# Dilated window attention and a maxout feed-forward layer: one unit of the second batch, not four, turned by TensorE, steps of scores and values taken apart, and a first tile that opens on three chunks of four

## The chip, the cores and the metric

The kernel runs on one core of one Trainium2 chip. The metric is the time of one execution on the device in microseconds (us). Beside it stands one execution taken by the hardware profiler, with a trace of every instruction on the five engines: TensorE (PE in the profile, its weight loads apart as PEld), VectorE (DVE), ScalarE (ACT), GpSimd (POOL) and SyncE (SP), which here only issues DMAs.

## The reference, cut to what matters

```python
# q, k, v: [8 batches, 8 heads, 576 positions, 64]; 4 heads plain, 4 dilated
scores = q @ k.T / 8
rel = pos[:, None] - pos[None, :]
mask_plain = (rel >= 0) & (rel < 32)                       # heads 0-3
mask_dil = (rel >= 0) & (rel < 128) & (rel % 4 == 0)       # heads 4-7
attn = softmax(where(mask, scores, -1e9))                  # denominator + 1e-9
x = (attn @ v) with the heads side by side                 # [8*576 = 4608, 512]
h = max(x @ w1, x @ w2, x @ w3)                            # 512 -> 768
out = h @ w_out                                            # 768 -> 512
```

All is float32. Only a band of scores counts, 32 keys per query, so the kernel computes small blocks beside the diagonal.

## The kernel before, in words

**The feed-forward layer.** The 4608 tokens are cut into nine tiles of 512. Each number is kept as a high part in the fp32r format and a low remainder, and each product is made of three (`ffn`, L957): high weights by high x, high weights by low x, low weights by high x. A tile has 18 "up" groups (six blocks `f` of 128 hidden columns, three weights each). A group is 12 matmuls into one PSUM bank `u`: three steps of four matmuls, one for each 128-row chunk of x (L979 to L987). The four chunks are the four pairs of heads. VectorE takes the maximum over the three groups (`tmp`), ScalarE rounds it to `h`, GpSimd makes the remainder. Then 72 "down" matmuls into the banks `d` (L1034) give four blocks of 128 tokens. So a tile is 216 up and 72 down matmuls of 512 columns.

**The weights** come once. `weight` (L394) loads an up group (512 KB) or half a down block (256 KB) into a staging tile `st`, and ScalarE, GpSimd and VectorE make the high and low parts `wupH`, `wupL` and `wdn` from packed bytes (L456 to L483).

**Attention** works in units: batch `b`, pair of heads `p` (0 and 1 plain, 2 and 3 dilated), 32 in all. There are two ways to make one:

- `full(b, p)` (L488), used for the first `NPAIR * FULL` = 8 units, the two first batches. TensorE writes the mask into the score banks `fs` with four matmuls of an identity (L553) and adds 36 or 48 score products (L559). VectorE takes row maxima (L576), and for the first head of the pair the subtraction (L579) and the sum (L585) too; ScalarE makes the exponentials (L582, L599); GpSimd normalises `W`. TensorE turns `W` in three steps of transposes (`ft`, L643 and L667), ScalarE copies the result out (`PT`), and 36 or 48 products with the values (`fpv`, L689) give x.
- `attention(u)` (L765) with `behind` (L814), for the other 24. 40 or 48 score products (`s`, L801), mask, maximum and shift in one custom VectorE operation for each of ten blocks (L830), exponentials and sums on ScalarE (L842), normalising on GpSimd, and 12 or 16 VectorE transposes of 32x32 blocks (L891). 32 products with the values (`pv`, L929) follow.

In both, x is copied to `xH` and its remainder to `xL` (ScalarE and VectorE). In the second way, `products` (L940) makes one TensorE step of the values of a unit and the scores of the next (`unit`, L1075), so the two stand side by side on TensorE.

**The order of all work** is computed when the kernel is built, by `Plan` (L104). Each step has a cost for each engine that may do it. `deadlines` gives each a due time, counted back from the feed-forward steps, which are numbered through at a pace; `order` (L171) then always takes the step that can begin first, by due time among those, and so fixes each engine's queue. Engines work their queues strictly in that order. TensorE steps of the first tile wait for all four chunks of x of batch 0. While TensorE would wait, `filler` matmuls (`idle`, L1116) are put in before the first feed-forward step; one of the two banks tagged `ffn` serves them until then, and the first value bank of every `full` unit has that tag too (L681). Loads stand in SP's queue by the same rule, the two `k` buffers in turn; the third unit of the first batch has its keys and queries in spare `h` buffers.

A tile needs x of all units of its tokens: the first tile batch 0, the second batches 0 and 1, and so on. The units of batch 1 are therefore worked on while the first tile runs.

Of the kernel before, what the change touches and what calls it, by code (L numbers as in the profile page):

```python
# [21 lines left out]
HALF = 288  # L22
# [24 lines left out]
FILL = 0.22  # L47
PER_BLOCK = 0.146
BACKLOG = 4.0
WEIGHT_PACE, WEIGHT_SLACK, WEIGHT_LEAD = 0.3, 3.188, 0.8  # L50

# [39 lines left out]
class Step:  # L91


    def __init__(self, costs, fn, bufs, nbytes, rows, kind, lead):
        self.costs, self.fn, self.bufs, self.nbytes, self.rows = costs, fn, bufs, nbytes, rows
        self.kind, self.lead = kind, lead
        self.usual = self.eng = next(iter(costs))
        self.next = []
        self.left = 0
        self.goal = self.due = 0.0  # L100
        self.ready = dict.fromkeys(costs, 0.0)


class Plan:  # L104
# [10 lines left out]
    def __init__(self):  # L115
        self.steps, self.made, self.given = [], {}, {}
        self.kind, self.lead = None, 0.0

    def add(self, costs, fn, deps=(), bufs=(), nbytes=0, rows=128):
# [51 lines left out]
    def order(self, fill=None):  # L171
# [14 lines left out]
        while len(order) - fills < len(self.steps):  # L186
            best = None
            for e, cands in waiting.items():
                now = free[e]
                for st in cands:  # L190
                    at = max(now, st.ready[e], wire - BACKLOG if e == "sp" else 0.0)
                    if best is not None and at > best[0]:
                        continue
                    if st.bufs:
                        at = max(at, self.room(st, slots))
                    if best is not None and (at, st.due) >= best[:2]:
# [10 lines left out]
                    best = (at, st.due, e, st)  # L207
            at, _, e, st = best
            assert at < 1e9, "the steps wait for each other's buffers"
            if e == "pe" and st.kind == "ffn" and len(slots["ffn"]) < 2 and fill:  # L210
                fill = None
# [67 lines left out]
def tile_dilated_window_attention__then__maxout_ffn(  # L279
# [114 lines left out]
    def weight(j, before):  # L394
# [56 lines left out]
        def sign(_):  # L451
# [36 lines left out]
    def full(b, p):  # L488
# [5 lines left out]
        top = 64 + nq  # L494
        at_h = not b and p == 2
        kb = buf("h" if at_h else "k", f"fk{b}{p}", [128, 1024] if at_h else None, F32)
# [13 lines left out]
        if at_h:  # L510
            ks = plan.add(*load(kb, qk[b, p % 2, :, 576:], 128, nkc))
            qs = plan.add(*load(qb, qk[b, p % 2, :, :576], 128, 576))
        else:
            ks = qs = plan.add(*load(kb, qk[b, p % 2], 128, 576 + nkc))
        if b:
# [31 lines left out]

        def scores(_):

            for j in range(2):  # L550
                for i, g in enumerate((slice(0, 4 * dil or 1), slice(4 * dil or 1, G))):
                    m = steps[:, i : i + 1, :wk].broadcast_to([128, g.stop - g.start, wk])
                    nc.tensor.matmul(S3(j)[:, g], identb, m, start=not i, stop=False, skip_group_check=True)  # L553
            for n, (r, i) in enumerate(blocks):
                q0, k0 = 144 * r + nq * i, ko + kw * r + nq * i
                for j in range(2):
                    d = slice(64 * j, 64 * j + 64)
# [9 lines left out]

        s = plan.add({"pe": 0.6 + 1.05}, scores, [ks, qs, first_of[b]], [*{kb, qb}, mx, *banks])
        expd = []
        for j, bank in enumerate(banks):  # L570
# [20 lines left out]

            t = plan.add({"dve": dve(nw)}, most, [s], [bank, mx])
            if byblock:
# [41 lines left out]
        for j in range(2):  # L635
# [21 lines left out]
            normed.append(t)  # L657
            t = plan.add({"pe": 4 * gw / 600 + 0.05}, flip, [t], [W, flips[j], *PT])
            copied.append(plan.add({"act": act(8 * nq), "dve": dve(8 * nq)}, moved, [t], [flips[j], PT[j]]))
# [8 lines left out]

        s = plan.add({"pe": (4 * gw if dil else 2 * nq) / 600 + 0.05}, rest, normed, [W, flips[2]])
        for j in range(2):  # L670
# [28 lines left out]
        for z in range(2):  # L699
# [20 lines left out]
            ls.append(l)  # L720
        return [(2 * HALF * b, 2 * HALF * b + 2 * HALF, hs, ls)]

    def rounded_of(b, p, dil, pv):

        def rounded(s):
            out = []
            for z, (c0, c1) in enumerate(((0, 256), (256, 2 * HALF))):
# [4 lines left out]
                for a, e in ((x0, wrap), (wrap, x1)):  # L732
# [26 lines left out]
                    ls.append(l)  # L759
                out.append((x0, x1, hs, ls))  # L760
            return out
# [3 lines left out]
    def attention(u, after):  # L765
# [30 lines left out]
        def scores():  # L796
# [11 lines left out]

        cost = sum(nq * SCORE for _, _, nq, *_ in blocks)
        return (scores, cost, [kload], [kb, mx, W, *banks]), (  # L810
            lambda s: behind(u, name, s, blocks, banks, W, mx, sm, v, vloads)
        ), (kload, last)

    def behind(u, name, s, blocks, banks, W, mx, sm, v, vloads):  # L814
# [40 lines left out]
        blank = [None, None]  # L855
        if u < NPAIR * FULL + 2:
            blank = [
# [78 lines left out]

        cost = 4 * (2 * HALF / 2400 + 8 * 0.0105)
        return values, cost, [*vloads, *turned[0], *turned[1]], [*v, *PT, *pv], rounded_of(b, p, dil, pv)

    def products(units, scores=()):  # L940
# [3 lines left out]
        def run(_):  # L944
# [3 lines left out]
        s = plan.add(  # L948
            {"pe": sum(x[1] for x in parts) + 0.25},
            run,  # L950
# [6 lines left out]
    def ffn(t0, n, x_of, w_of, prev):  # L957
# [12 lines left out]

        hs, hsteps = [], []
        for f in range(NF):
            tmp, hb = buf("tmp", f"tmp{t0}_{f}"), buf("h", f"h{t0}_{f}")
            for g in range(3):
                bank = buf("ffn", f"u{t0}_{f}_{g}")
                terms = ((wupH, 0, 0), (wupH, 0, 1), (wupL, 1, 0))
                for m, (wt, wz, xz) in enumerate(terms):

                    def up(_, m=m, wt=wt, xz=xz, f=f, g=g, bank=bank):  # L979
                        for c in range(4):  # L980
                            nc.tensor.matmul(  # L981
                                sums(bank),
                                wt[:, 3 * f + g, c, :],
                                moving(xL if xz else xH, c),
                                start=(m == 0 and c == 0),
                                stop=(m == 2 and c == 3),
                            )  # L987

                    prev = plan.add(
                        {"pe": 4 * (n * 0.000425 + 0.01)},  # L990
                        up,
                        [
                            prev,
                            *(x for a in x_of if a[0] < t0 + n and a[1] > t0 for x in a[2 + xz]),
                            w_of[3 * f + g][wz],
                        ],
                        [bank],
                    )
                if g == 0:
# [75 lines left out]
    def unit(u):  # L1075
# [109 lines left out]
```

## Time and profile before

| | us |
|---|---|
| median of 3 runs | 710.59 (709.3 to 713.65) |
| the profiled execution, its own time | 709.76 |
| its span, first to last instruction | 708.0 |
| TensorE busy in the span | 697.6 |
| VectorE, ScalarE, GpSimd busy | 330.9, 251.9, 178.7 |

A row of a timeline or of the chain has the start, the duration, the engine, the line, the tiles (`out<-in`) and the number of instructions merged. A row of a table of stretches has, for each engine, busy time and number of instructions, then the granted clock of TensorE as a share of full speed, the share of the DMA engines and GB/s. Ends of matmuls are modelled: what a matmul costs in a stream is read from one start to the next. "idle before <-releaser" names what ended a wait.

### The profile page before, as it was taken

The page shows a single profiled execution, that of the slowest core. Times are in us where ns is not written, and L with a number is a line of the kernel's source. Part 1 is how long each engine was busy: PE and PEld are TensorE (multiplying, and loading weights), DVE is VectorE, ACT ScalarE, POOL GpSimd, SP SyncE. Part 2 cuts the span into 40 slices and gives each one's busy share as a digit, 9 for nine tenths or more (in the row PEclk, how much of TensorE's full clock was granted, in tenths as well). Part 3 has the DMA queues.
Part 4 walks back from the last instruction along what each step waited for, and adds up shares of the span by engine and source line. Part 5 has one row for each costly group of instructions (what it writes and reads, how often), then busy time and mean ns, then how long its engine had stood idle before and what let it go on. Part 6 is the DMA issues. An engine that isn't in the chain of part 4 may idle for free.

```text
span 708.0 us, 13566 instructions
## 1 busy us (share of the span) xinstructions
PE 697.6 (99%) x5253; PEld 565.2 (80%) x5253; DVE 330.9 (47%) x1188; ACT 251.9 (36%) x875; POOL 178.7 (25%) x236
## 2 busy tenths in 40 slices
PE   9989999999999999999999999999999999999997
PEld 5668778888888888888888888888888888888886
DVE  6889754565555554513455544555455301101110
ACT  5857743333333333312433333334333211111111
POOL 3666752122112221211122211221122101100120
PEclk9999999999999999999999999999999999999999
DMA  9991822221221213100321032112200010010001
GB/s 298 330 375 58 243 72 106 75 61 64 89 92 62 65 64 119 59 1 24 137 80 57 11 109 77 59 62 94 92 26 1 16 44 1 0 45 16 0 1 59
DMA packets 23407, 57.42 MB, mean 81 GB/s; under 512 B 3056, under 2 KB 4784, under 8 KB 23344
## 3 DMA queue, kind: packets, MB, share of 16 engines
q1 hardware_dynamic: 23344, 56.57, 24.2%
q8 instruction: 41, 0.67, 0.4%
q14 instruction: 22, 0.18, 0.1%
HBM read 47.12 MB, written 9.44 MB: 80 GB/s over the span
## 4 chain that ended last, share of the span: by engine, by line
PE 92%; DMA 4%; POOL 2%; DVE 1%; issue 1%; ACT 0%; SPq 0%; POOLq 0%; ACTq 0%
PE u L981 61%; PE d L1036 21%; PE pv L929 4%; PE s L801 3%; DMA fk<-in_qk_p_dram 1%; DMA st<-in_w_dn_dram 1%; DMA st<-in_w_up_dram 1%; POOL W L371 1%; PE fpv L689 1%; PE fs L559 0%; PE idle L1117 0%; POOL wdn L371 0%; DVE fmx L576 0%; PE ft L643 0%; POOL c L438 0%
## 5 line engine op out<-in xcount | busy, mean ns | idle before, releaser
L981 PE MATMUL u<-xH,wupH 128*128 128x512 f32 x648 | 176.3, 394 | 2.0 <-ACT tmp L347 1.8
L981 PE MATMUL u<-xL,wupH 128*128 128x512 f32 x648 | 174.8, 391 | 0.0
L371 DVE TENSOR_TENSOR tmp<-u,tmp 128x512 f32<-128x512 f32 x108 | 74.5, 690 | 213.8 <-PE u L981 207.7
L981 PE MATMUL u<-xH,wupL 128*128 128x512 f32 x648 | 173.8, 390 | 0.0
L1036 PE MATMUL d<-wdn,h 128*128 128x512 f32 x648 | 151.4, 391 | 0.0
L371 POOL TENSOR_TENSOR h<-tmp,h 128x512 fp32r<-128x512 f32 x54 | 69.8, 1293 | 310.9 <-ACT h L347 310.6
L981 PEld LDWEIGHTS u<-xH,wupH 128*128 128x128 f32 x648 | 121.0, 189 | 28.4 <-ACT tmp L347 2.3
L981 PEld LDWEIGHTS u<-xH,wupL 128*128 128x128 f32 x648 | 121.4, 188 | 25.5
L981 PEld LDWEIGHTS u<-xL,wupH 128*128 128x128 f32 x648 | 121.2, 188 | 25.6
L1036 PEld LDWEIGHTS d<-wdn,h 128*128 128x128 f32 x648 | 120.8, 188 | 25.9
L891 DVE STREAM_TRANSPOSE PT<-W 32x256 f32<-32x256 f32 (+1 forms) x336 | 117.7, 350 | 27.8 <-POOL W L371 21.9
L842 ACT ACTIVATE W<-W,mx 128x96 f32<-128x96 f32 (+2 forms) x240 | 85.6, 359 | 38.1 <-DVE mx L830 38.1
L347 ACT CAST h<-tmp 128x512 fp32r<-128x512 f32 x54 | 33.5, 621 | 183.9 <-DVE tmp L371 183.9
L830 DVE CUSTOM_DVE_ANT_0 W<-s,steps 128x96 f32<-128x96 f32 x192 | 37.1, 253 | 58.5 <-PE s L801 58.5
L347 ACT COPY tmp<-u 128x512 f32<-128x512 f32 x54 | 31.7, 587 | 62.3 <-POOL h L371 34.4
L371 POOL TENSOR_TENSOR W<-W,sm 128x768 f32<-128x768 f32 (+2 forms) x48 | 44.2, 920 | 34.5 <-DVE sm L876 34.5
L347 ACT COPY o<-d 128x512 f32<-128x512 f32 x36 | 21.2, 588 | 79.9 <-PE d L1036 77.8
L842 ACT ACTIVATION_READ_ACCUMULATOR W<-W,mx 128x1 f32 (+1 forms) x240 | 45.3, 189 | 0.0
L871 POOL TENSOR_TENSOR sm<-sm,small_c 128x8 f32<-128x8 f32 (+2 forms) x48 | 9.4, 195 | 136.0 <-ACT W L842 136.0
L347 ACT CAST xH<-pv 128x320 fp32r<-128x320 f32 (+3 forms) x46 | 16.3, 381 | 65.5 <-PE pv L929 47.5
L929 PEld LDWEIGHTS pv<-PT,v 96*64 96x64 f32 (+2 forms) x768 | 26.3, 137 | 8.5 <-issue 6.7
L929 PE MATMUL pv<-PT,v 96*64 96x64 f32 (+2 forms) x768 | 29.9, 230 | 0.0
(70 smaller groups left out, 408.8 us busy)
## 6 DMA issues: line engine op xcount, KB each, us to landing
st<-in_w_up_dram SPq DMA_DIRECT2D x18, 512.0 KB, 9.0
out_dram<-o SPq DMA_DIRECT2D x36, 256.0 KB, 2.0
k<-in_qk_d_dram SPq DMA_DIRECT2D x12, 640.0 KB, 4.2
k<-in_qk_p_dram SPq DMA_DIRECT2D x12, 592.0 KB, 4.5
st<-in_w_dn_dram SPq DMA_DIRECT2D x12, 256.0 KB, 4.8
v<-in_vb_p_dram SPq DMA_DIRECT2D x12, 256.0 KB, 4.3
v<-in_vb_d_dram SPq DMA_DIRECT2D x12, 224.0 KB, 4.3
fk<-in_qk_p_dram SPq DMA_DIRECT2D x4, 592.0 KB, 7.3
```

The lines of the kernel that those rows point to most:

```text
L347: nc.scalar.copy(dst, src)
L371: (nc.vector if eng == "dve" else nc.gpsimd).tensor_tensor(dst, a, b, op=op)
L689: nc.tensor.matmul(pv[z].t[64 * j : 64 * j + 64, c : c + nq], value(n, j), PT[j].t[:wk, x : x + nq], start=True, stop=True,)
L801: nc.tensor.matmul(banks[j].t[o : o + nq, 96 * m : 96 * m + nk], kb.t[d, q0 : q0 + nq], kb.t[d, k0 : k0 + nk], start=True, stop=True,)
L830: nc.vector.tensor_tensor_reduce(W.t[:rows, a], banks[j].t[:rows, 96 * m : 96 * m + nk], tails[:rows, :nk] if m == 4 else steps[:, 0 if di ...
L842: nc.scalar.activation(W.t[:rows, a], W.t[:rows, a], AF.Exp, bias=mx.t[:rows, n : n + 1], scale=-1.0, accum_out=sm.t[:rows, n : n + 1],)
L871: nc.gpsimd.tensor_tensor(d, d, eps_c[:rows].broadcast_to([rows, n]), op=ALU.add)
L891: plan.add({"dve": dve(32 * n) + 0.02}, lambda _: nc.vector.transpose(dst(), src()), [*deps, blank[z]], [W, PT[z]])
L929: nc.tensor.matmul(pv[z].t[64 * j : 64 * j + 64, q0:q1], v[z].t[:rows, j, m, :], rows_of(z)[:rows, 4 * j + m, : q1 - q0], start=True, stop ...
L981: nc.tensor.matmul(sums(bank), wt[:, 3 * f + g, c, :], moving(xL if xz else xH, c), start=(m == 0 and c == 0), stop=(m == 2 and c == 3),)
L1036: nc.tensor.matmul(bank.t, hs[f].t[:, hz, s0 : s0 + 128], wdn[f].t[:, wz], start=(f == 0 and m == 0), stop=(f == NF - 1 and m == 2),)
```

## The change

It has four parts.

1. `FULL_UNITS = 5` takes the place of `NPAIR * FULL` = 8: only unit 0 of batch 1 still goes through `full`. Units 5, 6 and 7 (pairs 1, 2 and 3 of batch 1) are made as the later ones are.
2. `ALONE = 10`: for units 5 to 9 the values are a TensorE step of their own, and not joined with the next unit's scores.
3. `PORDER = (2, 0, 1, 3)`: in batch 0 the dilated pair 2 comes first. Its keys and queries come as two transfers of 64 partitions each, one for each head, and each head's scores are a step of their own that waits for its half alone. Pair 1 is now the one in the `h` buffers. The first two up groups of the first tile are made of the chunks 2, 0 and 1 first (nine matmuls each), and of chunk 3 later (three each), so they can begin before pair 3 is done; the step that opens the feed-forward layer takes the second `ffn` bank, and the value banks of batch 1 and of pair 3 no longer have the `ffn` tag. Chunks are summed in the order 2, 0, 1, 3 everywhere.
4. The planner: the first three up weights get a fixed due time (`RANK_ST`), a step that could begin up to `HOLD` later may be preferred by due time, and most costs and paces have new values.

The diff, cut to its core (the steps' new names `ups`, `early` and `scored` are at the places named above):

```diff
-SPILL = 1.67
+SPILL = 1.342
-SCORE = 0.00105
-FFN_PACE = 1.044
-UNIT_PACE, UNIT_SLACK, UNIT_LEAD = 1.271, 7.676, 3.484
+SCORES, VALUES = 1.06, 1.14
+FFN_PACE = 1.081
+UNIT_PACE, UNIT_SLACK, UNIT_LEAD = 1.319, 7.676, 3.484
-PER_BLOCK = 0.146
-BACKLOG = 4.0
-WEIGHT_PACE, WEIGHT_SLACK, WEIGHT_LEAD = 0.3, 3.188, 0.8
+PER_BLOCK = 0.131
+FLIP = 0.00088
+BACKLOG = 4.768
+HOLD = 0.102
+WEIGHT_PACE, WEIGHT_SLACK, WEIGHT_LEAD = 0.204, 3.188, 0.509
...
+FULL_UNITS = 5
+PORDER = (2, 0, 1, 3)
+FIRST_ST, RANK_ST = 3, -27.563
+EARLY = PORDER
+ALONE = 10
...
-            st.goal = st.due = g - k * dur
+            st.goal = g - k * dur
+            st.due = st.goal if st.rank is None else st.rank
...
+        if j < FIRST_ST:
+            s.rank = RANK_ST + j
...
+            for d in ([slice(0, 64), slice(64, 128)] if first_unit else [slice(0, 128)]):
+                def keys_in(_, d=d):
+                    nc.sync.dma_start(out=kb.t[d, : 576 + nkc], in_=qk[b, p % 2, d])
...
+        if first_unit:
+            scored = [plan.add({"pe": 0.25 + 1.1}, lambda _, j=j: scores([j]), [heads[j]], [kb, mx, banks[j]]) for j in range(2)]
...
-        pv = [buf("b" if i else "ffn", f"fpv{b}{p}_{i}") for i in range(2)]
+        pv = [buf("b" if i or b or p == PORDER[3] else "ffn", f"fpv{b}{p}_{i}") for i in range(2)]
...
-        if u < NPAIR * FULL + 2:
+        if u < FULL_UNITS + 2:
             blank = [
...
+        def ups(f, g, bank, chunks, opens=False):
+            for m, (wt, wz, xz) in enumerate(((wupH, 0, 0), (wupH, 0, 1), (wupL, 1, 0))):
+                def up(_, m=m, wt=wt, xz=xz):
+                    for c in chunks:
+                        nc.tensor.matmul(
...
+                            start=(m == 0 and c == EARLY[0]),
+                            stop=(m == 2 and c == EARLY[3]),
...
+        ahead = 2 if not t0 else 0
+        early = [buf("ffn", f"u{t0}_0_{g}") for g in range(ahead)]
+        for g, bank in enumerate(early):
+            ups(0, g, bank, EARLY[:3], g == 1)
...
+                if f == 0 and g < ahead:
+                    bank = early[g]
+                    ups(f, g, bank, EARLY[3:])
...
         made = [rest(s)] if new else []
+        if u < ALONE:
+            for r in products(made)[1]:
+                x_of.extend(r())
+            made = []
...
-                if u < NPAIR * FULL:
+                if u < FULL_UNITS:
                     plan.lead = UNIT_LEAD * (NPAIR - 1 - p)
-                    x_of.extend(full(u // NPAIR, p))
+                    x_of.extend(full(u // NPAIR, p if u >= NPAIR else PORDER[p]))
                 else:
-                    if u == NPAIR * FULL:
+                    if u == FULL_UNITS:
                         unit(u)
                     unit(u + 1)
```

More of the change, by code (lines that the diff above doesn't have):

```diff
@@ L100, in __init__ @@
         self.goal = self.due = 0.0
+        self.rank = None
         self.ready = dict.fromkeys(costs, 0.0)
@@ L188, in order @@
             for e, cands in waiting.items():
-                now = free[e]
+                now, found, soon = free[e], [], 1e9
                 for st in cands:
                     at = max(now, st.ready[e], wire - BACKLOG if e == "sp" else 0.0)
-                    if best is not None and at > best[0]:
+                    if at > soon + HOLD:
                         continue
-                    if st.bufs:
+                    if st.bufs and not (fill and st is self.opener):
                         at = max(at, self.room(st, slots))
-                    if best is not None and (at, st.due) >= best[:2]:
+                    if at > soon + HOLD:
                         continue
@@ L206, in order @@
                             continue
-                    best = (at, st.due, e, st)
+                    soon = min(soon, at)
+                    found.append((st.due, at, st))
+                found = [x for x in found if x[1] <= soon + HOLD]
+                if found:
+                    due, at, st = min(found, key=lambda x: x[:2])
+                    if best is None or (at, due) < best[:2]:
+                        best = (at, due, e, st)
             at, _, e, st = best
             assert at < 1e9, "the steps wait for each other's buffers"
-            if e == "pe" and st.kind == "ffn" and len(slots["ffn"]) < 2 and fill:
+            if st is self.opener and fill:
                 fill = None
@@ L494, in full @@
         top = 64 + nq
-        at_h = not b and p == 2
+        at_h, first_unit = not b and p == PORDER[2], not b and p == PORDER[0]
         kb = buf("h" if at_h else "k", f"fk{b}{p}", [128, 1024] if at_h else None, F32)
@@ L511, in full @@
             ks = plan.add(*load(kb, qk[b, p % 2, :, 576:], 128, nkc))
+            heads = []
             qs = plan.add(*load(qb, qk[b, p % 2, :, :576], 128, 576))
         else:
-            ks = qs = plan.add(*load(kb, qk[b, p % 2], 128, 576 + nkc))
+            ks = qs = None
+            heads = []
+            for d in ([slice(0, 64), slice(64, 128)] if first_unit else [slice(0, 128)]):
+                def keys_in(_, d=d):
+                    nc.sync.dma_start(out=kb.t[d, : 576 + nkc], in_=qk[b, p % 2, d])
+                heads.append(plan.add({"sp": 0.5}, keys_in, (), [kb], (d.stop - d.start) * (576 + nkc) * 4))
         if b:
@@ L546, in S3, with scores @@
             return banks[j].t[:, :nw].rearrange("p (n k) -> p n k", k=wk)
-        def scores(_):
-            for j in range(2):
+        def scores(js):
+            for j in js:
                 for i, g in enumerate((slice(0, 4 * dil or 1), slice(4 * dil or 1, G))):
@@ L555, in scores @@
                 q0, k0 = 144 * r + nq * i, ko + kw * r + nq * i
-                for j in range(2):
+                for j in js:
                     d = slice(64 * j, 64 * j + 64)
@@ L566, in scores @@
                     )
-        s = plan.add({"pe": 0.6 + 1.05}, scores, [ks, qs, first_of[b]], [*{kb, qb}, mx, *banks])
+        if first_unit:
+            scored = [plan.add({"pe": 0.25 + 1.1}, lambda _, j=j: scores([j]), [heads[j]], [kb, mx, banks[j]]) for j in range(2)]
+        else:
+            scored = 2 * [
+                plan.add({"pe": 0.47 + 1.08}, lambda _: scores(range(2)), [ks, qs, *heads, first_of[b]], [*{kb: 0, qb: 0}, mx, *banks])
+            ]
         expd = []
@@ L590, in eighth @@
                 )
-            t = plan.add({"dve": dve(nw)}, most, [s], [bank, mx])
+            t = plan.add({"dve": dve(nw)}, most, [scored[j]], [bank, mx])
             if byblock:
@@ L657, in full @@
             normed.append(t)
-            t = plan.add({"pe": 4 * gw / 600 + 0.05}, flip, [t], [W, flips[j], *PT])
+            t = plan.add({"pe": 4 * gw * FLIP + 0.06}, flip, [t], [W, flips[j], *PT])
             copied.append(plan.add({"act": act(8 * nq), "dve": dve(8 * nq)}, moved, [t], [flips[j], PT[j]]))
@@ L667, in rest @@
                     nc.tensor.transpose(flips[2].t[:wk, c : c + rows], W3(j)[:rows, g], ident[:rows, :rows])
-        s = plan.add({"pe": (4 * gw if dil else 2 * nq) / 600 + 0.05}, rest, normed, [W, flips[2]])
+        s = plan.add({"pe": (4 * gw if dil else 2 * nq) * FLIP + 0.06}, rest, normed, [W, flips[2]])
         for j in range(2):
@@ L759, in rounded @@
                     ls.append(l)
-                out.append((x0, x1, hs, ls))
+                out.append((x0, x1, p, hs, ls))
             return out
@@ L807, in scores @@
                     )
-        cost = sum(nq * SCORE for _, _, nq, *_ in blocks)
-        return (scores, cost, [kload], [kb, mx, W, *banks]), (
+        return (scores, SCORES, [kload], [kb, mx, W, *banks]), (
             lambda s: behind(u, name, s, blocks, banks, W, mx, sm, v, vloads)
@@ L935, in values @@
                         )
-        cost = 4 * (2 * HALF / 2400 + 8 * 0.0105)
-        return values, cost, [*vloads, *turned[0], *turned[1]], [*v, *PT, *pv], rounded_of(b, p, dil, pv)
+        return values, VALUES, [*vloads, *turned[0], *turned[1]], [*v, *PT, *pv], rounded_of(b, p, dil, pv)
     def products(units, scores=()):
@@ L948, in products @@
         s = plan.add(
-            {"pe": sum(x[1] for x in parts) + 0.25},
+            {"pe": sum(x[1] for x in parts) + 0.05},
             run,
@@ L971, in ffn @@
         hs, hsteps = [], []
+        def ups(f, g, bank, chunks, opens=False):
+            nonlocal prev
+            j = 3 * f + g
+            for m, (wt, wz, xz) in enumerate(((wupH, 0, 0), (wupH, 0, 1), (wupL, 1, 0))):
+                def up(_, m=m, wt=wt, xz=xz):
+                    for c in chunks:
+                        nc.tensor.matmul(
+                            sums(bank),
+                            wt[:, j, c, :],
+                            moving(xL if xz else xH, c),
+                            start=(m == 0 and c == EARLY[0]),
+                            stop=(m == 2 and c == EARLY[3]),
+                        )
+                prev = plan.add(
+                    {"pe": len(chunks) * (n * 0.000425 + 0.01)},
+                    up,
+                    [
+                        prev,
+                        *(x for a in x_of if a[0] < t0 + n and a[1] > t0 and a[2] in chunks for x in a[3 + xz]),
+                        w_of[j][wz],
+                    ],
+                    [bank],
+                )
+                if opens and not m:
+                    plan.opener = prev
+        ahead = 2 if not t0 else 0
+        early = [buf("ffn", f"u{t0}_0_{g}") for g in range(ahead)]
+        for g, bank in enumerate(early):
+            ups(0, g, bank, EARLY[:3], g == 1)
         for f in range(NF):
@@ L974, in ffn @@
             for g in range(3):
[L975 to L998, printed above, removed]
+                if f == 0 and g < ahead:
+                    bank = early[g]
+                    ups(f, g, bank, EARLY[3:])
+                else:
+                    bank = buf("ffn", f"u{t0}_{f}_{g}")
+                    ups(f, g, bank, EARLY)
                 if g == 0:
```

3 lines of the change are left out of this document (2 added, 1 removed).

## The prediction

> **What bounds the kernel now.** First the page: how much of the span the busiest engine fills, and the chain of waits.
>
> ```profile
> span 708.0 us, 13566 instructions
> PE 697.6 (99%) x5253; PEld 565.2 (80%) x5253; DVE 330.9 (47%) x1188; ACT 251.9 (36%) x875; POOL 178.7 (25%) x236
> PE 92%; DMA 4%; POOL 2%; DVE 1%; issue 1%; ACT 0%; SPq 0%; POOLq 0%; ACTq 0%
> ```
>
> TensorE is the bound, and 92% of the chain that ended last is its own work. The rest (DMA, POOL) must lie in one place, so next the chain in order of time.
>
> ```profile
> 106.77 1.18 PE pv L929 x32
> ...
> 122.88 1.18 PE pv L929 x32
> ...
> 128.10 13.62 PE u L981 x60
> ...
> 212.41 1.17 PE pv L929 x32
> 213.59 1.07 PE s L801 x47
> 214.65 15.63 PE u L981 x68
> ...
> 573.37 48.99 PE u L981 x216
> 622.36 16.35 PE d L1036 x72
> ```
>
> From 128 us on, where the second tile starts, one TensorE stretch follows the other without a gap. A tile costs 48.99 + 16.35 = 65.34 us, 0.2268 us a matmul. A later attention unit costs 1.17 + 1.07 = 2.24 us. The 68 matmuls after it take 15.63 us, 0.21 more than 68 x 0.2268: that is the price of going from small products back to large ones, about **0.2 us a visit**. So behind 128 us only TensorE instructions can be saved, and all else is decided ahead of it. The table of stretches shows that part.
>
> ```profile
> 34.10:98.30 64.20, 60.87 (x582) 47.85 (x577) 50.85 (x123) 46.78 (x147) 42.85 (x57) 0.97 0.61 200
> 98.30:127.90 29.60, 29.60 (x262) 24.16 (x261) 17.04 (x80) 10.08 (x41) 7.37 (x11) 1.00 0.33 109
> ```
>
> The first tile starts at 34.1 us. Until 98.3 us all engines are crowded: TensorE 95%, VectorE (third group of numbers) 50.85 of 64.2 = 79%. After it VectorE falls to 58%: there is room, but only 30 us of it.
>
> **Part one: three units change their way.** TensorE's small work in the crowded stretch is that of the four units of batch 1:
>
> ```profile
> L689 PE MATMUL fpv<-PT,fv 80*64 80x48 f32 (+1 forms) x168 | 5.8, 224 | 0.0
> L643 PE MATMUL ft<-ident,W 128*96 128x128 f32 (+1 forms) x32 | 5.0, 280 | 1.3 <-POOL W L371 1.0 <-ACT W L599 0.3
> L559 PE MATMUL fs<-fk 64*48 64x80 f32 (+1 forms) x137 | 3.5, 237 | 0.0
> L667 PE MATMUL ft<-ident,W 112*80 112x112 f32 (+1 forms) x12 | 2.1, 297 | 0.0
> L553 PE MATMUL fs<-steps,identb 128*128 128x320 bf16 (+3 forms) x12 | 1.8, 269 | 0.0
> ```
>
> Removed are pairs 1, 2 and 3. Values: 132 of 168 products, 5.8 x 132/168 = 4.6. Transposes: three quarters of 7.1 = 5.3; some 0.6 of that, by estimate, is the slow clock shown below and is counted there, so 4.7. Scores: the unit that stays had its masks and nearly all of its products before 34.1 us, so nearly all of 3.5 + 1.8, 5.2. That is 14.5 busy; busy time counts the overlapped ends of some 14 merged groups, so I take 12.3 plus nine visits of 0.2: **-14.1**. Added are three units of 2.24 and six visits of 0.2, since scores and values now stand apart: **+7.9**. Units 8 and 9 taken apart add two visits, **+0.4**. Net **-5.8 us** on TensorE. If steps apart fall beside each other in the queue anyway, up to 1.0 less.
>
> The waits in that stretch belong to the removed steps:
>
> ```profile
> 41.83 1.20 PE L981 MATMUL u<-xH,wupH 128*128 128x512 f32 x4 [1.83 <-ACT tmp L347]
> ...
> 84.70 0.55 PE L643 MATMUL ft<-ident,W 112*80 112x112 f32 x4 [0.34 <-ACT W L599]
> ...
> 89.39 0.58 PE L643 MATMUL ft<-ident,W 112*80 112x112 f32 x4 [0.98 <-POOL W L371]
> ```
> ```profile
> 90.00:92.00 2.00, 2.00 (x52) 1.95 (x53) 0.98 (x3) 0.92 (x4) 1.84 (x4) 0.91 0.19 36
> 92.00:94.00 2.00, 2.00 (x9) 1.81 (x8) 0.82 (x2) 2.00 (x10) 2.00 (x4) 0.50 0.69 224
> 94.00:96.00 2.00, 2.00 (x8) 1.53 (x8) 0.00 (x0) 2.00 (x12) 0.36 (x2) 0.74 0.04 11
> ```
>
> The dilated units' transposes wait 0.34 and 0.98 us. Then the granted clock (the number before the DMA share) falls to 0.91, 0.50 and 0.74: 2 x (0.09 + 0.50 + 0.26) = 1.7 us lost. Both go with those transposes: **-3.0 us**; bounds -3.0 and 0, as other waits may bring the same clock. The 1.83 us at 41.8 (a copy late behind weight work in ScalarE's queue) I leave; bounds 0 and -1.8.
>
> The Trainium skill, "TensorE: Matmul & The Clock Gate" (Loop structure matters more than you think, and the table above it), asks only that TensorE not pause for more than about 3 us. By that rule a new wait of 1 us would cost just itself; in the rows here a wait of 0.98 us among small matmuls was followed by half clock, so a new wait is reckoned at up to 2.7 us.
>
> **Part two: what VectorE gets.** Its price of each way:
>
> ```profile
> L891 DVE STREAM_TRANSPOSE PT<-W 32x256 f32<-32x256 f32 (+1 forms) x336 | 117.7, 350 | 27.8 <-POOL W L371 21.9
> L830 DVE CUSTOM_DVE_ANT_0 W<-s,steps 128x96 f32<-128x96 f32 x192 | 37.1, 253 | 58.5 <-PE s L801 58.5
> L830 DVE DVE_READ_ACCUMULATOR2_ANT mx<- 128x1 f32 (+1 forms) x240 | 19.8, 83 | 0.0
> L830 DVE CUSTOM_DVE_ANT_0 W<-s,tails 64x64 f32<-64x64 f32 (+1 forms) x48 | 8.6, 206 | 0.0
> L576 DVE TENSOR_REDUCE fmx<-fs 128x5 f32<-128x480 f32 (+1 forms) x16 | 10.0, 649 | 3.5 <-PE fs L559 3.5
> L371 DVE TENSOR_TENSOR W<-fs,fmx 128x480 f32<-128x480 f32 x8 | 5.2, 649 | 0.0
> L585 DVE TENSOR_REDUCE fsm<-W 128x5 f32<-128x480 f32 (+1 forms) x8 | 5.1, 640 | 0.0
> ```
>
> New way: 183.2/24 = 7.6 us a unit. Old way: 20.3/8 = 2.5. The copies of x are alike. So three units add **15.3 us of VectorE** ahead of the second tile, which needs all of batch 1. VectorE did 50.85 + 17.04 = 67.9 us between 34.1 and 128 us; with the addition 83.2. But units 8 and 9, whose values stand at 106.8 and 122.9 us, aren't needed until the third tile: put off, they take 15.2 us back, and 68.0 remain. They then take their TensorE time, 4.9 us with visits, behind the second tile's start. That defines the test: **with the units put off, the time is unchanged if the second tile starts at 128 - 4.9 = 123 us**, and VectorE must then be 68.0/89 = 76% busy. For a time 8.9 lower it must start at 114 us, at 68.0/80 = 85%. Has VectorE kept up such a rate with these same steps?
>
> ```profile
> 50.00:60.00 10.00, 10.00 (x91) 8.01 (x90) 9.47 (x18) 7.91 (x22) 5.12 (x7) 1.00 0.55 184
> 60.00:70.00 10.00, 10.00 (x67) 7.95 (x69) 9.59 (x21) 7.42 (x24) 7.18 (x10) 1.00 0.08 28
> ```
>
> Yes: 95% for 20 us with TensorE never idle. So 85% over 80 us can be had, with little to spare; I take **+2 us** of new waits, with bounds 0 and +12.
>
> The Trainium skill, "VectorE: DVE Perf Modes" (Rules for kernel authors), speaks against this part: it would have TensorE do 128x128 transposes where the result may lie in PSUM. By TensorE's and VectorE's transposes alone (7.1 us for four units against 117.7 for 24) the trace agrees; the sum by that rule is the slower rival's.
>
> **Part three: the start.**
>
> ```profile
> 4.64 1.01 PE L553 MATMUL fs<-steps,identb 128*128 128x96 bf16 x4
> 5.58 1.36 PE L559 MATMUL fs<-fk 64*64 64x96 f32 x36
> 6.98 1.22 DVE L576 TENSOR_REDUCE fmx<-fs 128x5 f32<-128x480 f32 x2 [3.53 <-PE fs L559]
> ...
> 29.18 1.46 PE L1117 MATMUL idle<-identb 128*128 128x512 bf16 x6
> 30.70 1.70 PE L689 MATMUL fpv<-PT,fv 80*64 80x48 f32 x48
> 32.33 0.58 PE L553 MATMUL fs<-steps,identb 128*128 128x96 bf16 x4
> ...
> 34.12 1.32 PE L981 MATMUL u<-xH,wupH 128*128 128x512 f32 x4
> ```
>
> VectorE's chain begins at 6.98 us behind both heads' scores. With one head's at a time it begins at least half of the 36 products earlier, 0.65 us, besides a shorter transfer. Before the last values TensorE turns out 1.5 us of filler; after the change 18 early matmuls (4.1 us) stand ready when the third pair is done, so that this filler becomes work. The 1.8 us of scores after it is work already. **-2.1 us**; bounds 0 and -4.1. SP issues one transfer more, at about the 0.4 us of its others, beside those in flight: nothing. The new wait, the opening step's for the third pair's x, holds up pair 3's transposes behind it on TensorE if that pair is late. The first weights' new place in SP's queue I cost at nothing, since loads then run ahead of use; with the cover gone it is one more wait like that at 41.8, 1.8 us.
>
> **The sum.** -5.8 - 3.0 - 2.1 + 2.0 = -8.9 on the profiled execution's 709.76: 700.9. The median of the runs is 0.8 higher, which would give 701.7. I predict **701.5 us**, with 698 to 705 as the forecast's own range. A measurement of this kernel can tell about 1% (7.1 us) from no change, so faster means under 703.5.
>
> **Rivals.**
> 1. *The saving comes back as waiting for VectorE.* At the 79% of the crowded stretch, 68.0 us need 86: the second tile starts at 120, and the time is 709.8 - 8 + 4.9 = **707**. For: 79% is what the stretch shows over 64 us. Against: the 95% over 20 us.
> 2. *Slower: VectorE's queue does not put off units 8 and 9.* Then 83.2 us at 79 to 85% need 98 to 105 us, the second tile starts at 132 to 139 us, and the time is **714 to 721**. It decides once 83.2 us don't fit into 94, above 89% busy. For: both units' values come ahead of the second tile now, before their need. Against: the second tile's x is due a tile sooner.
> 3. *More is won:* also the 1.8 at 41.8 us, a start 4.1 earlier, no new waits: -5.8 - 3.0 - 4.1 - 1.8 = -14.7, **695**.
> 4. *The early groups don't start early* (x of the third pair comes no sooner than that of the fourth did): the start's term falls away, **703.6**; this is counted into the forecast's edge.
>
> **Chances.** Forecast 0.53 (of it 0.45 under 703.5, with 4 in its other 0.08), rival 1 0.23, rival 2 0.09, rival 3 0.15. Faster 0.45 + 0.15 = 0.60; within 1% 0.08 + 0.23 = 0.31; slower 0.09. The range goes from 694 to 711: it leaves out the slower rival and a little below.
>
> **What would show it.** Right: the second tile's first `u` at about 114 us; `fs`, `ft` and `fpv` of batch 1 at a quarter; no half clock near 92 us; the first `u` near 32 us with nine matmuls a group; VectorE about 85% busy up to the second tile. Wrong: TensorE idle before the second tile behind a VectorE transpose or `xL`, with a clock below 1; values of unit 8 ahead of the second tile; a first `u` still at 34 us.

## The result, and the profile after

The changed kernel took 701.1 us (median of four runs, 700.95 to 701.61), against 710.8 before (median of four): a ratio of **0.986, 95% interval 0.983 to 0.989**. The forecast was 701.5. The time fits closely; two of the four terms behind it don't, and they cancel: that the sum fits so well is luck.

The head of the page after, and the chain of waits by engine:

```profile
span 699.1 us, 13503 instructions
PE 692.2 (99%) x5174; PEld 561.7 (80%) x5174; DVE 346.2 (50%) x1277; ACT 251.1 (36%) x884; POOL 181.5 (26%) x244
PE 97%; DVE 2%; DMA 1%; issue 0%; ACT 0%; ACTq 0%; DVEq 0%
```

TensorE has 5.4 us less to do, VectorE 15.3 us more, just the 15.3 of the forecast. TensorE's share of the chain rose from 92 to 97%: that of transfers fell from 4 to 1%, and GpSimd's 2% is gone. All that TensorE still waits for (us in total, times, longest):

```profile
PE idle L1166 <- DVE identb L369: 1.7, 1, 1.7
PE ft L698 <- DVE W L387: 1.0, 1, 1.0
PE fs L585 <- DMA fk<-in_qk_d_dram: 0.5, 1, 0.5
```

The first and the last lie in the first 5 us, the middle one at 23.7 us. Behind the first up matmul there is none, where before there were 1.83, 0.34 and 0.98 us. The table of stretches, from the first tile to the second, and the order there in the chain:

```profile
34.10:98.30 64.20, 64.17 (x573) 51.09 (x571) 55.05 (x158) 44.75 (x136) 47.16 (x64) 1.00 0.59 191
34.00:116.00 82.00, 81.97 (x767) 65.33 (x764) 69.28 (x224) 52.55 (x167) 49.47 (x68) 1.00 0.57 184
```
```profile
90.62 1.18 PE pv L959 x32
...
96.60 1.07 PE s L832 x40
...
104.71 1.17 PE pv L959 x32
105.88 1.07 PE s L832 x40
...
113.29 1.17 PE pv L959 x32
...
115.35 1.07 PE s L832 x47
116.42 12.92 PE u L1010 x56
129.34 1.18 PE pv L959 x32
```

The clock stays at 1.00 in this part and TensorE is full. VectorE is busy 69.28 of 82 us, 84%; the forecast asked for 85. The second tile starts at 116.4 us (forecast 114, before 128.1). Ahead of it stand the values of units 5, 6 and 7 only; those of unit 8 come at 129.3 us. So the values of units 8 and 9 were put off, as supposed, and so were their transposes on VectorE. Their scores were not: the three `s` rows are units 8, 9 and 10, all ahead of the second tile.

The start, with the first up matmuls:

```profile
30.15 1.90 PE L1166 MATMUL idle<-identb 128*128 128x512 bf16 x8
31.70 1.04 PE L1010 MATMUL u<-xH,wupH 128*128 128x512 f32 x3
...
35.93 1.60 PE L720 MATMUL fpv<-PT,fv 80*64 80x48 f32 x48
37.47 0.97 PE L1010 MATMUL u<-xL,wupH 128*128 128x512 f32 x3
...
39.48 1.04 PE L585 MATMUL fs<-fk 64*64 64x96 f32 x36
40.45 0.50 PE L1010 MATMUL u<-xH,wupH 128*128 128x512 f32 x1
```

They begin at 31.7 us, 2.4 earlier than before, with three matmuls a step as meant. The filler that they were to replace is still there, just ahead of them (`idle`). And the last pair's values end at 37.5 us, where they ended at 32.3, and the scores of batch 1's first unit come behind them. So the earlier first matmul is no gain by itself. At 40.45 us the same work is done as before at 34.12, and 18 early matmuls (4.1 us) more: **the start is 40.45 - 4.1 - 34.12 = 2.2 us behind, not 2.1 ahead.**

### The profile page after: what moved, and what is told of

The parts are those of the page before. It is cut to its first block, busy times and chain, and to the rows that moved or that the text cites. A ratio compares the mean times of both kernels' runs of the same rounds, so it can differ in the third digit from the quotient of the medians.

```text
span 699.1 us, 13503 instructions
## 1 busy us (share of the span) xinstructions
PE 692.2 (99%) x5174; PEld 561.7 (80%) x5174; DVE 346.2 (50%) x1277; ACT 251.1 (36%) x884; POOL 181.5 (26%) x244
## 4 chain that ended last, share of the span: by engine, by line
PE 97%; DVE 2%; DMA 1%; issue 0%; ACT 0%; ACTq 0%; DVEq 0%
PE u L1010 64%; PE d L1081 21%; PE pv L959 5%; PE s L832 4%; PE fs L585 1%; PE fpv L720 1%; PE idle L1166 1%; DMA fk<-in_qk_d_dram 1%; DVE fmx L607 0%; PE ft L674 0%; DVE W L387 0%; PE fs L579 0%; DVE cp L460 0%; DVE cp L449 0%; DVE fsm L650 0%
## 5 line engine op out<-in xcount | busy, mean ns | idle before, releaser
L921 DVE STREAM_TRANSPOSE PT<-W 32x256 f32<-32x256 f32 (+1 forms) x380 | 132.6, 349 | 20.6 <-POOL W L387 13.7
L1010 PEld LDWEIGHTS u<-xL,wupH 128*128 128x128 f32 x648 | 120.8, 188 | 25.2
L872 ACT ACTIVATE W<-W,mx 128x96 f32<-128x96 f32 (+1 forms) x270 | 96.1, 359 | 38.9 <-DVE mx L860 38.9
L860 DVE CUSTOM_DVE_ANT_0 W<-s,steps 128x96 f32<-128x96 f32 x216 | 41.8, 252 | 58.7 <-PE s L832 58.6
L387 POOL TENSOR_TENSOR W<-W,sm 128x768 f32<-128x768 f32 (+2 forms) x53 | 49.4, 933 | 39.1 <-DVE sm L906 37.0
L363 ACT COPY tmp<-u 128x512 f32<-128x512 f32 x54 | 31.7, 587 | 64.2 <-POOL h L387 33.4
L872 ACT ACTIVATION_READ_ACCUMULATOR W<-W,mx 128x1 f32 x270 | 50.9, 189 | 0.0
L363 ACT CAST xH<-pv 128x320 fp32r<-128x320 f32 (+3 forms) x52 | 17.7, 375 | 64.5 <-PE pv L959 48.7
L959 PEld LDWEIGHTS pv<-PT,v 96*64 96x64 f32 (+2 forms) x864 | 29.6, 137 | 9.5 <-issue 8.1
L959 PE MATMUL pv<-PT,v 96*64 96x64 f32 (+2 forms) x864 | 33.7, 231 | 0.0
```

The source lines that it names most:

```text
L363: nc.scalar.copy(dst, src)
L387: (nc.vector if eng == "dve" else nc.gpsimd).tensor_tensor(dst, a, b, op=op)
L860: nc.vector.tensor_tensor_reduce(W.t[:rows, a], banks[j].t[:rows, 96 * m : 96 * m + nk], tails[:rows, :nk] if m == 4 else steps[:, 0 if di ...
L872: nc.scalar.activation(W.t[:rows, a], W.t[:rows, a], AF.Exp, bias=mx.t[:rows, n : n + 1], scale=-1.0, accum_out=sm.t[:rows, n : n + 1],)
L921: plan.add({"dve": dve(32 * n) + 0.02}, lambda _: nc.vector.transpose(dst(), src()), [*deps, blank[z]], [W, PT[z]])
L959: nc.tensor.matmul(pv[z].t[64 * j : 64 * j + 64, q0:q1], v[z].t[:rows, j, m, :], rows_of(z)[:rows, 4 * j + m, : q1 - q0], start=True, stop ...
```

## The experiments

Each kernel is compared with the kernel before on the same chip, by the ratio of times; the changed kernel stands at 0.986.

**1. Part one undone: `FULL_UNITS = 8` in the changed kernel.**

```diff
-FULL_UNITS = 5
+FULL_UNITS = 8
```

> The changed kernel, but all four units of batch 1 turned by TensorE again (eight full units). Theory (the gain is TensorE work saved ahead of the second tile, and the waits that went with it): TensorE gets about 7 us of small products back, its transposes wait again for 1 to 3 us, the second tile starts near 128 us minus what the start saves, time 707 to 711. Rival (the new order of the start and the planner's numbers made the gain): 701 to 703.

708.5 us, ratio 0.998 (0.996 to 1.000): the other three parts without this one (part two then reaches units 8 and 9 only) are worth next to nothing, as the theory said. The second tile starts at 127.7 us, 11.4 later than in the changed kernel. Of that 2.8 are the values of units 8 and 9, which stand ahead of it again (at 114.4 and 122.6 us), 1.1 the scores of unit 11 (at 123.8 us), 1.7 waits of 0.46 and 1.25 us, and 0.3 a later start. The 5.5 that remain are the three units' small work and visits; the forecast had 14.1 - 7.9 = 6.2. That a changed kernel loses its gain when one part is taken back doesn't by itself show that this part made it: experiments 7 and 9 lose as much.

**2. Part one alone, in the kernel before.**

```diff
-        if u < NPAIR * FULL + 2:
+        if u < 5 + 2:
...
-                if u < NPAIR * FULL:
+                if u < 5:
...
-                    if u == NPAIR * FULL:
+                    if u == 5:
```

> The kernel before, with only the first of the four parts: five full units instead of eight; start, joined steps and all numbers of the planner as before. Theory (the units make the gain): about 7 us less TensorE work, the transposes' waits and the half clock near 92 us gone, 0 to 4 us of new waits since the numbers aren't fitted; first up matmul still at 34 us, second tile at 117 to 121 us, time 701 to 706. Rival (start and numbers make it): 708 to 712.

706.1 us, ratio 0.994 (0.992 to 0.996), at the theory's upper end. TensorE's four longest waits in all:

```profile
PE u L981 <- ACT tmp L347: 2.6, 2, 1.9
PE idle L1117 <- DVE identb L353: 1.7, 1, 1.7
PE ft L643 <- POOL W L371: 1.5, 2, 0.8
PE u L981 <- ACT xH L347: 1.3, 1, 1.3
```

The second tile starts at 120.8 us, so the TensorE time is saved. But in this order TensorE waits in many places, some of them still for transposes (`ft`), and the first up matmul slips to 37.4 us, where 34 was expected. Part one alone brings 0.6% of the 1.4.

**3. No early groups.**

```diff
-                if opens and not m:
+                if not (t0 or f or g or m):
                     plan.opener = prev
...
-        ahead = 2 if not t0 else 0
+        ahead = 0
```

> The changed kernel without the early groups: the first two up groups in one go, after all four pairs. Theory: in the changed kernel the last pair's x is ready only near 39 us, against 34 before, and TensorE has some 4 us of other small work from 31.7 us on, so without the 18 early matmuls it stands idle or fills for up to 4 us more: first up matmul at 35 to 39 us, time 703 to 706. Rival (the early groups only swap places with the last pair's transposes and values, and save nothing): 700.5 to 702.

702.4 us, ratio 0.989 (0.985 to 0.993); the interval overlaps the changed kernel's. The last pair is served sooner when nothing is put before it:

```profile
34.01 1.60 PE L720 MATMUL fpv<-PT,fv 80*64 80x48 f32 x48
35.55 1.21 PE L1010 MATMUL u<-xH,wupH 128*128 128x512 f32 x4
```

Its values come 1.9 us earlier than with the early groups. So these mostly trade places with the last pair: about 1 us, not told from nothing. The result lies between theory and rival, nearer to the rival.

**4. VectorE's limit: each transpose of units 5 to 7 done twice, order unchanged.**

```diff
-plan.add(..., lambda _: nc.vector.transpose(dst(), src()), ...)
+plan.add(..., lambda _: [nc.vector.transpose(dst(), src()) for _ in range(2 if u < 8 else 1)], ...)
```

> The changed kernel in the same order, with each VectorE transpose of units 5, 6 and 7 done twice (the second writes the same again). That is 24 long and 20 short transposes more, 15 us of VectorE, where it is 69.3 us busy of the 82 us from 34 to 116 us. Theory (VectorE is near its limit there, with 12.7 us left): the 15 us don't all fit, TensorE waits ahead of the second tile, 3 to 12 us more, time 704 to 713. Rival (VectorE is far from setting the time): 701 to 702.

716.1 us, ratio 1.009 (1.006 to 1.012): about 15 us for 15 us of VectorE, more than the theory gave. Timeline of TensorE and the stretch with its clock:

```profile
112.37 1.33 PE L959 MATMUL pv<-PT,v 112*64 112x80 f32 x16 [3.89 <-DVE xL L387]
...
126.64 0.78 PE L959 MATMUL pv<-PT,v 112*64 112x80 f32 x16 [2.88 <-DVE xL L387]
```
```profile
111.00:118.00 7.00, 5.63 (x62) 4.58 (x63) 6.01 (x28) 2.87 (x14) 1.97 (x3) 0.52 0.19 69
...
128.00:132.00 4.00, 4.00 (x55) 3.07 (x54) 2.84 (x26) 3.25 (x15) 0.39 (x2) 0.57 0.36 116
```

The values wait for VectorE's queue, and with each such wait the clock is cut. TensorE is busy 5.63 us of the first stretch and all of the last, so that costs about 5.63 x 0.48 + 4 x 0.43 = 4.4 us besides the waiting itself. The second tile starts at 130.0 us. This is the load of the forecast's slower rival, brought about by other means: VectorE does 83.95 us of work from 34 to 130 us, where the rival had 83.2.

**5. The other direction: those transposes left out, order unchanged** (x of units 5 to 7 is then made from data that were not turned).

```diff
-plan.add(..., lambda _: nc.vector.transpose(dst(), src()), ...)
+plan.add(..., lambda _: [nc.vector.transpose(dst(), src()) for _ in range(0 if u < 8 else 1)], ...)
```

> The changed kernel in the same order, leaving out the VectorE transposes of units 5, 6 and 7 (x of these units is made from unturned data): 15 us of VectorE less ahead of the second tile. Theory (TensorE waits for nothing there in the changed kernel, VectorE is just fast enough): no gain, 699.5 to 701.5, where 15 us more cost 15. Rival (VectorE sets the time at this place already): 4 us or more less, under 697.

702.3 us, ratio 0.988 (0.985 to 0.991). VectorE is busy 53 us there, and nothing is won:

```profile
34.00:116.00 82.00, 81.32 (x735) 64.70 (x734) 53.06 (x176) 51.44 (x164) 49.52 (x68) 1.00 0.57 186
```

The traced execution gets going 1.3 us later, after waits of 1.6 us for keys in the first part. From its first long stretch of up matmuls (43.44 us, 42.15 in the changed kernel) to the second tile it takes 74.27 us, to the hundredth what the changed kernel takes. With experiment 4 this places the changed kernel at the edge: less VectorE work gains nothing, more costs in full.

**6. One step further: no unit of batch 1 turned by TensorE, `FULL_UNITS = 4`.**

```diff
-FULL_UNITS = 5
+FULL_UNITS = 4
```

> The changed kernel with no unit of batch 1 turned by TensorE (four full units). Theory (VectorE stands at its limit ahead of the second tile, where 15 us more of it cost 15 us): TensorE saves about 2.2 us, VectorE gets about 5 more, and 3 to 5 of these become TensorE's waits: 702 to 705. Rival (TensorE's work alone decides): 698 to 700.

704.3 us, ratio 0.992 (0.990 to 0.995). VectorE has 72.75 us to do in the 82, and ahead of the values of batch 1's second unit TensorE stands still:

```profile
34.00:116.00 82.00, 79.73 (x709) 64.14 (x701) 72.75 (x248) 52.25 (x172) 49.01 (x69) 1.00 0.54 184
```
```profile
96.63 1.46 PE L959 MATMUL pv<-PT,v 96*64 96x64 f32 x32 [2.27 <-issue]
```

The profile names no releaser for these 2.27 us. VectorE is busy 2.43 of the 2.6 us from 94.0 to 96.6, with this unit's last two groups of transposes (94.87 and 96.56 us) split by weight work; that its queue is behind the wait is argued from that, not shown. The traced execution took 702.0 us, the shortest of the seven, so the trace doesn't hold all of the loss.

**7. Part two undone: values and next scores joined again, `ALONE = 0`.**

```diff
-ALONE = 10
+ALONE = 0
```

> The changed kernel with the values of units 5 to 9 joined again with the next unit's scores. Theory (VectorE decides when the second tile can start): scores of unit 6 then wait for the values of unit 5, so VectorE gets the work of units 6 and 7 later and has to do it closer to the second tile; five visits of 0.2 us are saved, but TensorE waits: 702 to 708. Rival (only the number of visits counts): 700 to 701.

711.3 us, ratio 1.002 (1.000 to 1.004), past the theory's range: the whole gain is gone. The timeline of TensorE, and the table of stretches behind it:

```profile
97.01 0.47 PE L1081 MATMUL d<-wdn,h 128*128 128x512 f32 x1 [1.08 <-POOL sm L901]
100.29 1.22 PE L1081 MATMUL d<-wdn,h 128*128 128x512 f32 x2 [2.81 <-POOL wdn L387]
```
```profile
98.00:108.00 10.00, 7.46 (x84) 5.11 (x85) 9.02 (x31) 3.08 (x9) 5.74 (x10) 0.54 0.19 51
```

TensorE runs into down matmuls whose weights GpSimd has not made yet. The second wait names them; both together are 3.9 us. The clock is near one half for the 10 us from 98 us on; TensorE is busy 7.46 of them, so that costs about 7.46 x 0.46 = 3.4 more. The chain of waits passes these matmuls by: it runs through the normalising on GpSimd (97.08 us) and the transposes on VectorE (98.67 to 102.77 us) to the next values at 102.82 us. So VectorE is behind the delay too, as the theory had it; the trace doesn't price the two apart.

**8. Parts one and two in the kernel before**, to see whether steps apart help by themselves (the edit of experiment 2 and this one).

```diff
         made = [rest(s)] if new else []
+        if u < 10:
+            for r in products(made)[1]:
+                x_of.extend(r())
+            made = []
```

> The kernel before with the first two of the four parts: five full units, and units 5 to 9 in steps apart; start and numbers as before. With the first part alone it took 706.1. Theory (apart, the scores of units 6 and 7 run ahead of the values of the unit before, and VectorE gets its work earlier): scores of units 5 to 7 stand before the values of unit 5, 2 to 4 us less than with the first part alone, 702 to 704. Rival (joining hurt only through the changed numbers): 705.5 to 707.

706.1 us, ratio 0.994 (0.992 to 0.997), the same as with part one alone. **My theory fell here:** steps apart are worth nothing with the old start and numbers. So what experiment 7 lost comes from joined steps together with the rest of the changed kernel, not from joined steps as such. Whether the start or the numbers matter there was not tried.

**9. Most of part four undone: the planner's old numbers in the changed kernel.** The new costs of TensorE's steps (`SCORES`, `VALUES`, `FLIP`) stay.

```diff
-FIRST_ST, RANK_ST = 3, -27.563
+FIRST_ST, RANK_ST = 0, -27.563
-SPILL = 1.342
+SPILL = 1.67
-FFN_PACE = 1.081
+FFN_PACE = 1.044
-UNIT_PACE, UNIT_SLACK, UNIT_LEAD = 1.319, 7.676, 3.484
+UNIT_PACE, UNIT_SLACK, UNIT_LEAD = 1.271, 7.676, 3.484
-PER_BLOCK = 0.131
-BACKLOG = 4.768
-HOLD = 0.102
-WEIGHT_PACE, WEIGHT_SLACK, WEIGHT_LEAD = 0.204, 3.188, 0.509
+PER_BLOCK = 0.146
+BACKLOG = 4.0
+HOLD = 0.0
+WEIGHT_PACE, WEIGHT_SLACK, WEIGHT_LEAD = 0.3, 3.188, 0.8
```

> The changed kernel with the planner's numbers of before (paces, spill, backlog, no hold, no fixed rank for the first weights). Theory (units and start make the gain, the numbers only place steps): the same TensorE work, 1 to 5 us of new waits ahead of the second tile, 702 to 706. Rival (the numbers make most of it): 707 to 711.

707.8 us, ratio 0.998 (0.996 to 1.001): within the rival's range. TensorE's timeline, then the stretches:

```profile
99.96 0.35 PE L832 MATMUL s<-k 64*64 64x96 f32 x2 [1.99 <-issue]
101.56 1.92 PE L832 MATMUL s<-k 64*64 64x96 f32 x38 [1.25 <-DVE c L468]
```
```profile
100.00:102.00 2.00, 0.74 (x14) 0.58 (x18) 1.86 (x8) 0.41 (x1) 0.07 (x1) 0.65 0.02 7
102.00:104.00 2.00, 2.00 (x45) 1.60 (x41) 1.79 (x16) 0.95 (x6) 1.65 (x2) 0.50 0.04 8
```

Again there are two pauses ahead of the second tile, of 2.0 us (for which the profile names no releaser) and 1.3 us, and half clock behind them. The second tile starts at 122.2 us, 6 later than in the changed kernel.

**10. The first unit unsplit: one transfer, both heads' scores in one step.**

```diff
-at_h, first_unit = not b and p == PORDER[2], not b and p == PORDER[0]
+at_h, first_unit = not b and p == PORDER[2], False
```

> The changed kernel with the first unit (pair 2) loaded in one transfer and its scores in one step of both heads. Theory (the two halves of 64 partitions landed at 4.84 and 6.26 us, the whole of 128 before at 4.42; the products of one head alone take 74 ns each, those of two heads in turn less than half of it; so the split costs time at the start): both maxima can begin near 6.5 us instead of 6.8 and 9.05, the up matmuls start 1 to 2 us earlier, 699 to 701. Rival (the split is what makes the start early): 702 to 704.

702.8 us, ratio 0.990 (0.988 to 0.993); expected were 699 to 701, so the theory missed. What it said of the first microseconds came true:

```profile
4.64 0.90 PE L579 MATMUL fs<-steps,identb 128*128 128x320 bf16 x4
5.47 1.05 PE L585 MATMUL fs<-fk 64*48 64x80 f32 x48
6.45 0.39 PE L1166 MATMUL idle<-identb 128*128 128x512 bf16 x1
```

All three first units' scores are done at 9.9 us instead of 13.1 for the like ones. Yet the first up matmul comes at 32.4, not earlier. The planner also orders the loads anew here, and the chain names a transfer of weights up to 24 us; that the new order is the reason is argued, not shown:

```profile
12.69 11.26 DMA st<-in_w_up_dram
```

**11. The same order with one transfer for the two halves.**

```diff
-    nc.sync.dma_start(out=kb.t[d, : 576 + nkc], in_=qk[b, p % 2, d])
+    whole = slice(0, 128) if first_unit else d
+    if d.start == 0:
+        nc.sync.dma_start(out=kb.t[whole, : 576 + nkc], in_=qk[b, p % 2, whole])
```

> The changed kernel in the same order, the first unit's keys and queries loaded by one transfer of 128 partitions in place of the first half's, and no second transfer; scores still one head at a time. Theory (a transfer of 64 partitions takes about as long as one of 128: the halves landed at 4.84 and 6.26, the whole at 4.58 when unsplit): the first scores start no later and the second head's need no wait, but from 6 us on the DMA queues are full and the planner's order is unchanged, so the time stays at 700 to 701.5. Rival (the split gives the early start): first scores 0.5 us later or more and 702 or more.

701.0 us, ratio 0.987 (0.984 to 0.990), first up matmul at 31.68. Splitting the load does nothing. With experiment 10: an earlier beginning alone doesn't shorten the start.

**12. Only units 5 to 7 apart, `ALONE = 8`.**

```diff
-ALONE = 10
+ALONE = 8
```

> The changed kernel with only units 5 to 7 in steps apart; values of 8 and 9 joined with the next scores as for later units. Theory (steps apart help by letting VectorE begin on batch 1's units early; units 8 and 9 are not needed before the second tile): nothing waits more, two visits of 0.2 us are saved, 700 to 701.5. Rival (the order is so tight that any joined step costs): 703 to 708.

701.8 us (700.3 to 705.3), ratio 0.989 (0.986 to 0.992): not told from the changed kernel. No version tried beats that kernel by more than the noise.

## Why the prediction held, and where its steps failed

By stages, forecast and measurement:

| | forecast | measured |
|---|---|---|
| start, for the same work | -2.1 | +2.2 |
| from there to the second tile | -11.7 | -13.9 |
| behind the second tile's start (units put off) | +4.9 | +2.8 |
| sum | -8.9 | -8.9 |

The second row: before, 34.12 to 128.10 us, 94.0; after, 36.4 (the equal point) to 116.42, 80.0. The last row: 708.0 - 128.1 = 579.9 before, 699.1 - 116.4 = 582.7 after. That the sum agrees to a tenth is luck: the start was 4.3 us worse than forecast, the waits 3.85 better.

**TensorE's work, -5.8, was about right.** Rows two and three hold it with the waits, -11.1 together. Of that the waits that went are 1.83 + 0.34 + 0.98 = 3.15 and the clock 1.7, as the rows of before show; -6.2 remains for the work and the visits. Experiment 1 brings 5.5 back.

**The units put off, +4.9, were mis-sized.** The step was "they then take their TensorE time, 4.9 us with visits", which counts scores and values. Only the values of units 8 and 9 went behind the second tile's start: 2 x (1.18 + 0.2) = 2.8 us, which is what was measured. Their scores stayed ahead of it, 2.1 us that the forecast had put behind. The sum doesn't change by that.

**The waits, -3.0 with +2.0 of new ones, were mis-sized:** measured are -4.85 and no new ones. The step that failed is "I take +2 us of new waits", and beside it the copy at 41.8 us, which was left and went away. What helped to keep waits out, I had priced at nothing: the planner's numbers. With the old ones in the changed kernel the copy's wait is back (1.06 us at 41.5 us in experiment 9), new ones stand beside it, and the time is 707.8 us; with the new ones but without steps apart it is 711.3. Each of parts one and two and the numbers of part four, taken out of the changed kernel, costs 1.2 to 1.6%, while the whole is worth 1.4%; part one alone gives 0.6. These gains don't add up. My reading is that the units save the TensorE time, and that it only reaches the end if all queues are so ordered that nobody is late at this edge; which of the numbers does it was not tried.

**The start, -2.1, was wrong in sign.** The first step that failed was "it begins at least half of the 36 products earlier, 0.65 us, besides a shorter transfer". It began at 6.77 us, 0.2 earlier: one head's 24 products took 1.77 us here (0.97 at full clock, last section), where two heads' 36 took 1.30 before, and the half transfer landed no sooner than a whole one (last section). The second head's maximum could begin only at 9.05 us. The second was "this filler becomes work": 1.9 us of filler still stand ahead of the first up matmul. And I read the first up matmul as the start's end, while pair 3's work just moved behind it. Experiments 3, 10 and 11 show that the early groups, the first scores and the split load are each worth 1 to 2 us or nothing; the new order of the pairs, and part three as a whole, were not taken out by themselves. What bounds the start stays open between the full DMA queues and VectorE. In the changed kernel the chain of waits from 11.7 to 23.6 us is all VectorE's, which is busy 11.6 of 12 us there; in experiment 10 it is a transfer up to 24 us, and the DMA share is above 1 in both (changed kernel):

```profile
12.00:24.00 12.00, 11.03 (x181) 7.66 (x180) 11.62 (x24) 8.76 (x35) 7.94 (x9) 1.00 1.04 321
```

**VectorE's test, 85% up to the second tile, was the right one.** 84% was reached, though with unit 8's masks and maxima in it, which the forecast had put off. Experiments 4 and 5 show the edge from both sides, and that the slower rival was a real one: 15 us more of VectorE made 716.

## What to carry to other kernels

On a full engine, count what each unit costs it, and then ask of the engine that takes the work over how busy it must be up to the next due point; try it by doubling that work and by leaving it out in an unchanged order. When an earlier first instruction is the aim, compare the moment at which the same work is done, not the first instruction. An order that was fitted to one set of steps can lose the whole gain when one step is put back, so parts of such a change are not to be costed one by one.

## What the runs showed of the hardware

**A short wait can bring half clock with it, and doesn't always.** In experiments 4 and 9 waits of 1 to 4 us among small products, and in experiment 7 two among down matmuls, went with 3 to 10 us at about half clock. In experiment 9 the two waits of 1.99 and 1.25 us were enough, in the kernel before one of 0.98. But after 2.27 us in experiment 6, and after 1.83 us at 41.8 us in the kernel before, the clock stayed at 1.00, so the length of a wait alone doesn't decide. What does is open. The Trainium skill, "TensorE: Matmul & The Clock Gate" (the table above Loop structure matters more than you think), warns of pauses of about 3 us; here shorter ones did it.

**Products of one head alone run at half the rate.** The like products of pair 2, one head at a time, in experiment 12:

```profile
6.38 1.03 PE L585 MATMUL fs<-fk 64*48 64x80 f32 x24
7.35 0.58 PE L579 MATMUL fs<-steps,identb 128*128 128x96 bf16 x4
```
24 products of one head take 7.35 - 6.38 = 0.97 us there, at full clock as far as the durations show: the 36 products of two heads behind them take 0.97 us too, as at 12.13 us in the rows further down. In the rows of experiment 10, 48 of two heads take 6.45 - 5.47 = 0.98. The heads lie on the two halves of the partitions. The Trainium skill, "TensorE: Matmul & The Clock Gate" (Part 3: Packing small matmuls — row/col tiling), says that weight loads overlap running products only in other row groups, which fits these rows.

**The clock at the start.** In the changed kernel's profiled execution the same groups were slower still:

```profile
7.17 1.84 PE L585 MATMUL fs<-fk 64*48 64x80 f32 x24
8.94 0.98 PE L579 MATMUL fs<-steps,identb 128*128 128x96 bf16 x4
9.85 1.84 PE L585 MATMUL fs<-fk 64*64 64x96 f32 x36
11.61 0.58 PE L579 MATMUL fs<-steps,identb 128*128 128x96 bf16 x4
12.13 1.04 PE L585 MATMUL fs<-fk,fq 64*64 64x96 f32 x36
```

36 products took 1.76 us at 9.85 and 0.97 at 12.13. The rows of the clock say 1.00 there; these durations look like half clock up to about 11.5 us.

**A transfer of 64 partitions is no faster than one of 128.** The first half (320 KB) landed at 4.84 us, with the second half in flight behind it; in experiment 11 the whole (640 KB) landed at 4.80. A half with nothing behind it was not tried. The Trainium skill, "DMA: Bandwidth & Descriptors" (Rules for kernel authors), advises against splitting by halves of the partitions, since they share the same engines; the runs agree.
